# The first MLP's square on ScalarE, and the low parts of the weights' combinations a slot later

## The chip, the core and the metric

The kernel runs on one core of one Trainium2 chip. TensorE (PE in the profile) multiplies, with weight loads shown apart as PEld; VectorE (DVE) and ScalarE (ACT) do the elementwise work; all transfers are issued from the queue of SyncE (SP). The metric is the time of one execution on the device in microseconds (us), lower is better.

## The reference, cut to what matters

```python
batch, n_heads, seq, head_dim, n_pack = 8, 8, 576, 64, 32

p_packed = sm_attn(p, k, v)                    # softmax attention of 32 queries per head
out = sm_attn(q, p_packed, p_packed)           # all 576 positions on the 32 packed ones
x = out.transpose(0, 2, 1, 3).reshape(4608, 512)

h = np.maximum(x @ w_in, 0.0)                  # first MLP, 512 -> 2048 -> 512
x = h * h @ w_out

h = x @ w_in2                                  # second MLP, 512 -> 2048 -> 512
g = h * (1.0 / (1.0 + np.exp(-1.702 * h)))
return g @ w_out2
```

The weights arrive as 64-bit floats (read as int64 pairs of words), everything else as float32.

## The kernel before, in words

**Precision.** Each factor of a large product is kept as a high and a low part: the high part is a copy on ACT into a rounded type, the low part is the source minus the high part on DVE (`split`, lines 76 and 77). `prod` (line 85) then makes three matmuls for one product: high by high, high by low, low by high.

**First stage: attention and first MLP, by slots.** The batch of 8 is cut into halves of 288 positions (`HS`). One slot is one chunk `fc` of 128 of the 2048 hidden features, for one half of one batch: 256 slots in all (`SB`). In slot s the program is written in this order: `gsplit` of slot s+2 (high part on ACT, low part on DVE of the squared relu, tile `gh`), `mm1` of slot s+3 (six matmuls into the PSUM tile `h`, then the relu into `r` on ACT at line 381, then the square into `gf`), `mm2` of slot s (twelve matmuls that add to four accumulators `y`), and then what `plan[s]` holds. Every engine works through its own instructions in this order. `h` has two PSUM buffers, so `mm1` of slot s+5 can't start until all readers of `h` of slot s+3 are done. In slots 0 to 31 (batch 0) and 48 earliest slots in all the square is on ACT (line 384); in the other 208 it is on DVE (line 386), which reads `h` in PSUM a second time: max(h, 0) times r.

After the last chunk of a run (16 slots in most of the stage) the four accumulators are copied to `ysb`: those of even number on ACT (line 416), those of odd number on DVE (line 414). The next run's first `mm2` writes the same four accumulators. Two runs add to an earlier partial sum instead, all on DVE (line 412, `yp`).

**What else the plan holds.** For the next batch, spread over the slots: the packed attention (`s1`, `tr`, `pv`, `t2`), the second softmax for the two halves (`s2a`, `s2b`, `s2c`: transposes on DVE at line 330, maximum at 332, subtraction at 334, the exponential on ACT at 339, then lines 341, 343, 345, 347 and 350 on DVE, and the split of the result at 355 and 357), and four `m_step`, which multiply the packed values into `w_in` (high part on ACT at 366, low part on DVE at 368). So in each batch a half's softmax ends in the slots just before a run does. `interleave` writes out the first part of each planned step and then, in turns, what stands behind each `yield`.

**The second MLP's weights** are prepared in the same slots. Of each pair of 128-row blocks seven combinations of 256 columns are needed. `convert` loads and turns the 64-bit words into floats (lines 118 and 119 on ACT, 123 to 129 on DVE), `unit_sums` makes four sums (line 179), `unit_split` splits each combination into a tile `wc` (high at line 188 on ACT, low at line 190 on DVE) and writes it to DRAM (lines 193 and 195, 112 transfers of 256 KB). `wc` has two buffers. One unit takes eight slots of the list `calm`, which leaves out the slots with s % 16 of 14, 15 and 0, and starts at slot 45; its first slot has no split, the seven others have one each. SP issues these writes in the order of the program, between the loads of k, q, v, weights and raw words.

**Second stage.** The second MLP works on five pairs of column blocks with seven products in place of eight. It reads the weights that the first stage wrote, from slot 248 on; the last combination is made in slot 213.

Of the kernel before, what the change touches and what calls it, by code (L numbers as in the profile page):

```python
# [8 lines left out]
F32 = mybir.dt.float32  # L9
F32R = mybir.dt.float32r  # L10
# [3 lines left out]
AF = mybir.ActivationFunctionType  # L14
ALU = mybir.AluOpType
# [7 lines left out]
P = 128  # L23
HS = S // 2
# [19 lines left out]
def fused_kernel(ctx, tc, qT, kT, vv, pT, w_in, w_out, w_in2, w_out2, out):  # L44
# [7 lines left out]
    nc = tc.nc  # L52
# [26 lines left out]
    def prod(ps, ws, xs, start, stop, more=False):  # L79

        n = 3 * len(ws)
        i = 0
        for (wh, wl), (xh, xl) in zip(ws, xs):
            for w, x in ((wh, xh), (wh, xl), (wl, xh)):
                nc.tensor.matmul(ps, w, x, start=start and i == 0, stop=stop and i == n - 1,  # L85
                                 skip_group_check=more)
                i += 1
# [8 lines left out]
    cv_p = poola("cv", 3)  # L96
# [7 lines left out]
    s2_p = poola("s2", 1)  # L104
# [74 lines left out]
            nc.vector.tensor_tensor(out=t[:, o, :], in0=i0, in1=i1, op=op)  # L179
            yield  # L180

    def unit_split(u, i):

        xa, xb, t = xs[u, 0], xs[u, 1], xs[u, "s"]
        x = {1: xa[:, :256], 2: xb[:, :256], 3: t[:, 3, :], 4: xb[:, 256:], 5: t[:, 0, :], 6: t[:, 1, :], 7: t[:, 2, :]}[i]
        x = x.rearrange("p (c n) -> p c n", c=2)
        o = cv_p.tile([P, 2, 2, P], F32R, tag="o", name=f"wc{u}_{i}", bufs=2)
        nc.scalar.activation(o[:, :, 0, :], x, AF.Copy)
        yield
        nc.vector.tensor_tensor(out=o[:, :, 1, :], in0=x, in1=o[:, :, 0, :].bitcast(F32), op=ALU.subtract)  # L190
        if u < 8:
            q, d = divmod(u, 2)
            nc.sync.dma_start(out=w1_d[:, 2 * q:2 * q + 2, ORDER_A.index(i), d], in_=o.bitcast(F32))
        else:
            nc.sync.dma_start(out=w2_d[:, ORDER_B.index(i), u - 8], in_=o.bitcast(F32))
# [42 lines left out]
    def att_tile(b, alt, name):  # L238

        pool, tag = (mm_p, "mm") if b == 0 and alt else (at_p, "at")  # L240
        return pool.tile([P, 512], F32, tag=tag, name=name)

    def heads(ps, w, x):

        n = None
        for hp in range(4):
            for r in range(2):
                rows = slice(64 * r, 64 * r + 64)
                xx = x(hp)[rows]
                n = xx.shape[-1]  # L250
                nc.tensor.matmul(ps[r][32 * hp:32 * hp + 32, :n], w(hp)[rows], xx, start=True, stop=True)  # L251
# [69 lines left out]
    s2t = {}  # L321
    NB = HS // 32

    def s2a(b, hf):
        ps = [att_tile(b, False, f"s2_{b}_{hf}_{r}") for r in range(2)]
        heads(ps, lambda hp: ppT[b][:, 32 * hp:32 * hp + 32], lambda hp: qt[b, hp][:, hf * HS:(hf + 1) * HS])
        t = s2_p.tile([P, 2 * NB, 32], F32, tag="s2t", name=f"s2t{b}_{hf}", bufs=2)
        st = s2_p.tile([P, 3, 2 * NB, 1], F32, tag="s2st", name=f"s2st{b}_{hf}", bufs=2)
        for r in range(2):
            nc.vector.transpose(out=t[:, r * NB:(r + 1) * NB].rearrange("p n i -> p (n i)"), in_=ps[r][:, :HS])  # L330
            yield
        nc.vector.tensor_reduce(out=st[:, 0], in_=t, axis=AX.X, op=ALU.max)
        yield
        nc.vector.tensor_tensor(out=t, in0=t, in1=st[:, 0].to_broadcast([P, 2 * NB, 32]), op=ALU.subtract)
        s2t[b, hf] = t, st
# [37 lines left out]
    def mm1(b, hf, fc, seg):  # L373
        ps = mm_p.tile([P, 512], F32, tag="mm", name=f"h_{b}_{hf}_{fc}")
        m = M[b, fc // 4]
        c = slice((fc % 4) * P, (fc % 4 + 1) * P)
        a = A[b, hf]
        prod(ps[:, :HS], [(m[:, g, 0, c], m[:, g, 1, c]) for g in range(2)],
             [(a[:, g, 0, :], a[:, g, 1, :]) for g in range(2)], True, True)
        r = g_p.tile([P, HS], F32, tag="r", name=f"r_{b}_{hf}_{fc}")  # L380
        nc.scalar.activation(r, ps[:, :HS], AF.Relu)  # L381
        g = g_p.tile([P, HS], F32, tag="g", name=f"gf_{b}_{hf}_{fc}")
        if b < 1 or b < 2 and fc < 8:
            nc.scalar.activation(g, r, AF.Square)
        else:
            nc.vector.scalar_tensor_tensor(out=g, in0=ps[:, :HS], scalar=0.0, in1=r, op0=ALU.max, op1=ALU.mult)  # L386
        gf[b, hf, fc] = g

    def gsplit(b, hf, fc, seg):
# [221 lines left out]
    def run(item):  # L611
# [6 lines left out]
            (0, 0, 8, 15), (0, 1, 8, 15), (1, 0, 8, 15), (1, 1, 8, 15)]  # L618
    runs += [(b, hf, 0, NFC - 1) for b in range(2, B) for hf in range(2)]
    slots = [(mm1, gsplit, mm2, (b, hf, fc, (f0, f1))) for b, hf, f0, f1 in runs for fc in range(f0, f1 + 1)]  # L620
    SB = len(slots)
    plan = {s: [] for s in range(S0, len(slots))}
    plan_end = {s: 0 for s in plan}

    def at(s, f, *a):
        plan[s].append((f, a))
# [17 lines left out]
    def convert(s):  # L644

        nonlocal nconv
        n = nconv
        nconv += 1
        c, b, a = (cq[i] if 0 <= i < len(cq) else None for i in (n - 2, n - 1, n))
        if c:  # L650
            at(s, lambda: c["use"](c["x"]))
        if a:
            at(s, conv_a, a)
        if b:
            at(s, conv_b, b)
        if 0 <= n - 1 < len(cq):
            plan_end[s] += 1
# [21 lines left out]
    for f, *a in (*loads(0)[:6], (ahead,), loads(0)[6], (ahead,), (load_q, 0, 0, 0), (load_q, 0, 1, 0), (ahead,),  # L679
# [6 lines left out]
        -8: [(tr, 0, 1), (warm, 8), (convert,)],  # L686
        -7: [(convert,), (pv, 0, 0), (pv, 0, 1), (warm, 2), (t2, 0)],
        -6: [(convert,), (s2a, 0, 0)],
        -5: [(s2b, 0, 0), (convert,), (warm, 14)],
        -4: [(convert,), (s2a, 0, 1), (s2c, 0, 0), (warm, 14), (m_step, 0, 0)],  # L690
        -3: [(convert,)],
        -2: [(s2b, 0, 1), (convert,)],
# [7 lines left out]
        6: [(pv, 1, 0), (convert,), (tr, 1, 1)],  # L700
        7: [(convert,), (pv, 1, 1), (t2, 1)],
        8: [(s2a, 1, 0), (convert,)],
        9: [(s2b, 1, 0)],
        10: [(s2c, 1, 0), (convert,)],
# [28 lines left out]
    for b in range(1, B):  # L733
# [20 lines left out]
        for n in range(8):  # L754
            f = n // 2
# [5 lines left out]
    for u in range(2 * KC + 1):  # L761
        s = calm[8 * u:8 * u + 8]
        convert(s[0])
        convert(s[3])
        if u > 0:
            at(s[1], unit_sums, u - 1)
            for j, i in zip(s[1:], (2, 4, 1, 5, 6, 7, 3)):
                at(j, unit_split, u - 1, i)

    at(SB - 2 * NFC, open_b)  # L770

# [23 lines left out]
    for p in range(NP2):  # L795
        t0 = 2 * SL * p
        for c in range(KC):
            u = t0 + 7 * c
# [20 lines left out]
        for c in range(KC):  # L819
            u = t0 + 7 * c  # L820
# [5 lines left out]
        for n in range(14):  # L826
            i, h = ORDER_B[n // 2], n % 2
# [61 lines left out]
```

## Time and profile before

| | |
|---|---|
| Time, median of 3 runs | 1516.89 us (1514.85 to 1519.79) |
| Profiled execution, time | 1515.2 us |
| Profiled execution, span of its instructions | 1513.4 us |
| Granted TensorE clock, mean | 0.982 |
| PE busy | 1454.4 us (96%) |
| DVE busy | 1052.7 us (70%) |
| ACT busy | 760.6 us (50%) |

Busy time is that of instructions on the engine; the idle time of an engine is shown in front of the instruction that ended it, with what released that instruction. A granted clock of 1.00 is 2.4 GHz and 0.50 is 1.2 GHz; a stretch between the two had part of its time at either. Matmuls are pipelined, so their durations overlap.

### The profile page before, as it was taken

The page shows a single profiled execution, that of the slowest core. Times are in us where ns is not written, and L with a number is a line of the kernel's source. Part 1 is how long each engine was busy: PE and PEld are TensorE (multiplying, and loading weights), DVE is VectorE, ACT ScalarE, POOL GpSimd, SP SyncE. Part 2 cuts the span into 40 slices and gives each one's busy share as a digit, 9 for nine tenths or more (in the row PEclk, how much of TensorE's full clock was granted, in tenths as well). Part 3 has the DMA queues.
Part 4 walks back from the last instruction along what each step waited for, and adds up shares of the span by engine and source line. Part 5 has one row for each costly group of instructions (what it writes and reads, how often), then busy time and mean ns, then how long its engine had stood idle before and what let it go on. Part 6 is the DMA issues. An engine that isn't in the chain of part 4 may idle for free.

```text
span 1513.4 us, 25199 instructions
## 1 busy us (share of the span) xinstructions
PE 1454.4 (96%) x9786; PEld 1305.6 (86%) x9786; DVE 1052.7 (70%) x1892; ACT 760.6 (50%) x1552; POOL 0.7 (0%) x6
## 2 busy tenths in 40 slices
PE   7899999899899998999999999999999999999998
PEld 4678988888788888888999888888888889998997
DVE  6898477767768767685446678567757675876675
ACT  4888645445454554554345453454446344534542
POOL 0000000000000000000000000000000000000000
PEclk8899999999999999999999999999999999999999
DMA  8756647466465654643034576667656765675663
GB/s 301 244 175 220 208 165 228 153 221 217 141 214 175 205 185 160 230 136 121 17 143 162 199 259 245 226 211 273 237 207 236 273 223 198 250 267 212 218 243 145
DMA packets 110776, 307.97 MB, mean 203 GB/s; under 512 B 9024, under 2 KB 58176, under 8 KB 96576
## 3 DMA queue, kind: packets, MB, share of 16 engines
q1 hardware_dynamic: 110656, 306.35, 58.4%
q8 instruction: 77, 1.26, 0.3%
q14 instruction: 43, 0.35, 0.1%
HBM read 250.94 MB, written 55.38 MB: 202 GB/s over the span
## 4 chain that ended last, share of the span: by engine, by line
PE 75%; DVE 14%; ACT 4%; DMA 4%; issue 3%; SPq 0%; ACTq 0%; DVEq 0%
PE h L85 32%; PE y L85 20%; PE o L85 19%; DMA w_d<-wc 2%; PE m L251 2%; PE s L251 1%; DVE gh L77 1%; DVE gf L386 1%; DVE yT L480 1%; ACT g L515 1%; DVE y L491 1%; DVE T L510 1%; PE pv L309 1%; DVE M L368 1%; DVE s2t L347 1%
## 5 line engine op out<-in xcount | busy, mean ns | idle before, releaser
L85 PE MATMUL y<-gh,wo 128*128 128x288 f32 x3072 | 462.7, 300 | 17.0 <-DVE ysb L414 11.0
L85 PEld LDWEIGHTS y<-gh,wo 128*128 128x128 f32 x3072 | 433.1, 193 | 21.1 <-DVE ysb L414 12.5
L85 PE MATMUL h<-y,wA 128*128 128x464 f32 (+1 forms) x1680 | 355.6, 371 | 3.0 <-ACT r L553 2.9
L85 PE MATMUL o<-g,wB 128*128 128x464 f32 (+1 forms) x1680 | 354.6, 371 | 0.0
L85 PEld LDWEIGHTS h<-y,wA 128*128 128x128 f32 x1680 | 314.9, 188 | 40.5 <-ACT r L553 4.9
L85 PEld LDWEIGHTS o<-g,wB 128*128 128x128 f32 x1680 | 315.3, 188 | 35.6
L85 PE MATMUL h<-a,M 128*128 128x288 f32 x1536 | 267.0, 310 | 22.5 <-DVE gf L386 14.3
L85 PEld LDWEIGHTS h<-a,M 128*128 128x128 f32 x1536 | 223.4, 195 | 71.7 <-DVE gf L386 25.4
L76 ACT ACTIVATE gh<-gf 128x288 fp32r<-128x288 f32 x256 | 113.0, 442 | 93.8 <-DVE gf L386 93.1
L381 ACT ACTIVATE r<-h 128x288 f32<-128x288 f32 x256 | 103.3, 404 | 89.0 <-PE h L85 88.6
L77 DVE TENSOR_TENSOR gh<-gf,gh 128x288 fp32r<-128x288 f32 x256 | 115.0, 450 | 37.7 <-ACT gh L76 37.6
L561 DVE TENSOR_TENSOR hid<-h,r 128x464 f32<-128x464 f32 (+1 forms) x120 | 76.0, 634 | 77.5 <-PE h L85 66.4
L553 ACT ACTIVATE r<-h 128x464 f32<-128x464 f32 (+1 forms) x120 | 66.5, 554 | 119.3 <-PE h L85 119.3
L386 DVE SCALAR_TENSOR_TENSOR gf<-h,r 128x288 f32<-128x288 f32 x208 | 93.9, 451 | 45.8 <-ACT r L381 45.6
L515 ACT ACTIVATE g<-T 128x928 fp32r<-128x928 f32 (+1 forms) x60 | 58.5, 974 | 126.8 <-DVE T L510 119.7
L571 DVE TENSOR_TENSOR hid<-hid,sg 128x464 f32<-128x464 f32 (+1 forms) x120 | 75.7, 631 | 47.5 <-ACT sg L567 47.5
L491 DVE TENSOR_TENSOR g<-T,g 128x928 fp32r<-128x928 f32 (+1 forms) x60 | 66.7, 1118 | 53.3 <-ACT g L515 52.3
L491 DVE TENSOR_TENSOR g<-hid,g 128x928 fp32r<-128x928 f32 (+1 forms) x80 | 86.0, 1111 | 1.2 <-ACT g L515 1.1
L567 ACT ACTIVATE sg<-hid 128x464 f32<-128x464 f32 (+1 forms) x120 | 70.2, 585 | 30.7 <-DVE hid L561 30.7
L515 ACT ACTIVATE g<-hid 128x928 fp32r<-128x928 f32 (+1 forms) x80 | 74.3, 968 | 20.6 <-PE o L85 20.6
L368 DVE TENSOR_TENSOR M<-m,M 128x512 fp32r<-128x512 f32 x64 | 43.5, 687 | 40.1 <-ACT M L366 39.8
L510 DVE TENSOR_TENSOR T<-hid 128x928 f32<-128x928 f32 (+1 forms) x60 | 66.2, 1111 | 0.0
(97 smaller groups left out, 1022.8 us busy)
## 6 DMA issues: line engine op xcount, KB each, us to landing
wB<-w_d SPq DMA_DIRECT2D x70, 1024.0 KB, 4.7
wA<-w_d SPq DMA_DIRECT2D x40, 1024.0 KB, 4.7
wA<-w_d SPq DMA_DIRECT2D x40, 768.0 KB, 6.4
win<-win_d SPq DMA_DIRECT2D x56, 512.0 KB, 4.8
w_d<-wc SPq DMA_DIRECT2D x112, 256.0 KB, 2.6
k<-in_kT SPq DMA_DIRECT2D x32, 288.0 KB, 4.7
y_d<-ysb SPq DMA_DIRECT2D x16, 576.0 KB, 3.9
v<-in_vv SPq DMA_DIRECT2D x16, 512.0 KB, 5.9
```

What stands on the lines that cost most here:

```text
L76: nc.scalar.activation(hi, src, AF.Copy)
L77: nc.vector.tensor_tensor(out=lo, in0=src, in1=hi.bitcast(F32), op=ALU.subtract)
L85: nc.tensor.matmul(ps, w, x, start=start and i == 0, stop=stop and i == n - 1, skip_group_check=more)
L381: nc.scalar.activation(r, ps[:, :HS], AF.Relu)
L386: nc.vector.scalar_tensor_tensor(out=g, in0=ps[:, :HS], scalar=0.0, in1=r, op0=ALU.max, op1=ALU.mult)
L491: nc.vector.tensor_tensor(out=t[:, :, 1, :n], in0=src, in1=t[:, :, 0, :n].bitcast(F32), op=ALU.subtract)
L510: nc.vector.tensor_tensor(out=t, in0=i0, in1=i1, op=ALU.subtract)
L515: nc.scalar.activation(t[:, :, 0, :PAIRS[p]], gop[p, i, g, "src"], AF.Copy)
L553: nc.scalar.activation(t[:, 0, :n], bank[p, c, "1"][:, :n], AF.Copy)
L561: nc.vector.tensor_tensor(out=hid(p, c, blk), in0=bank[p, c, b][:, :n], in1=part[p, c, r][:, 0, :n], op=ALU.add)
L567: nc.scalar.activation(t, bank[p, c, "1"][:, :n] if blk == 2 else hid(p, c, blk), AF.Sigmoid, scale=GELU)
L571: nc.vector.tensor_tensor(out=hid(p, c, blk), in0=bank[p, c, "1"][:, :n] if blk == 2 else hid(p, c, blk), in1=part.pop((p, c, "sg", blk)), ...
```

## The change

The square of the first MLP is written as a Square activation of `r` on ACT, right behind the relu, in all 256 slots; before, 208 of them had it on DVE, reading `h` and `r`. The tile `wc` gets a third buffer. `unit_split` becomes two steps: `unit_hi` makes the high part in the slot where it was, `unit_lo` makes the low part and issues the write to DRAM in the slot behind it. Two tiles of the second softmax, `s2t` and `s2st`, go from two buffers to one, which makes room for the third `wc`.

```diff
-    def unit_split(u, i):
+    wcs = {}
+
+    def unit_hi(u, i):
 
         xa, xb, t = xs[u, 0], xs[u, 1], xs[u, "s"]
...
-        o = cv_p.tile([P, 2, 2, P], F32R, tag="o", name=f"wc{u}_{i}", bufs=2)
+        o = cv_p.tile([P, 2, 2, P], F32R, tag="o", name=f"wc{u}_{i}", bufs=3)
         nc.scalar.activation(o[:, :, 0, :], x, AF.Copy)
-        yield
+        wcs[u, i] = o, x
+
+    def unit_lo(u, i):
+        o, x = wcs.pop((u, i))
         nc.vector.tensor_tensor(out=o[:, :, 1, :], in0=x, in1=o[:, :, 0, :].bitcast(F32), op=ALU.subtract)
         if u < 8:
             q, d = divmod(u, 2)
...
-        t = s2_p.tile([P, 2 * NB, 32], F32, tag="s2t", name=f"s2t{b}_{hf}", bufs=2)
-        st = s2_p.tile([P, 3, 2 * NB, 1], F32, tag="s2st", name=f"s2st{b}_{hf}", bufs=2)
+        t = s2_p.tile([P, 2 * NB, 32], F32, tag="s2t", name=f"s2t{b}_{hf}", bufs=1)
+        st = s2_p.tile([P, 3, 2 * NB, 1], F32, tag="s2st", name=f"s2st{b}_{hf}", bufs=1)
...
         g = g_p.tile([P, HS], F32, tag="g", name=f"gf_{b}_{hf}_{fc}")
-        if b < 1 or b < 2 and fc < 8:
-            nc.scalar.activation(g, r, AF.Square)
-        else:
-            nc.vector.scalar_tensor_tensor(out=g, in0=ps[:, :HS], scalar=0.0, in1=r, op0=ALU.max, op1=ALU.mult)
+        nc.scalar.activation(g, r, AF.Square)
         gf[b, hf, fc] = g
...
             for j, i in zip(s[1:], (2, 4, 1, 5, 6, 7, 3)):
-                at(j, unit_split, u - 1, i)
+                at(j, unit_hi, u - 1, i)
+                at(j + 1, unit_lo, u - 1, i)
```

## Rows read from the trace of the kernel before

**Rows 1.** Windows: length, busy (and count) by engine, granted clock, DMA share, GB/s.

```profile
36.00:190.00 154.00, 141.73 (x1227) 125.15 (x1227) 118.90 (x251) 116.76 (x273) 0.00 (x0) 0.95 0.65 214
190.00:800.00 610.00, 581.19 (x4937) 532.11 (x4936) 422.49 (x986) 301.71 (x757) 0.00 (x0) 0.97 0.51 169
800.00:1513.40 713.40, 706.11 (x3381) 632.58 (x3379) 489.87 (x610) 327.38 (x493) 0.00 (x0) 1.00 0.62 226
...
120.00:160.00 40.00, 39.42 (x326) 35.79 (x327) 30.64 (x65) 33.01 (x80) 0.00 (x0) 1.00 0.76 246
```

**Rows 2.** Groups, 190 to 800 us: busy, mean ns; idle before, releasers.

```profile
L85 PE MATMUL y<-gh,wo 128*128 128x288 f32 x2504 | 376.7, 300 | 14.3 <-DVE ysb L414 11.0 <-ACT gh L76 3.2
...
L85 PE MATMUL h<-a,M 128*128 128x288 f32 x1242 | 211.5, 306 | 14.5 <-DVE gf L386 14.3
...
L386 DVE SCALAR_TENSOR_TENSOR gf<-h,r 128x288 f32<-128x288 f32 x208 | 93.9, 451 | 45.8 <-ACT r L381 45.6
L76 ACT ACTIVATE gh<-gf 128x288 fp32r<-128x288 f32 x208 | 91.9, 442 | 93.5 <-DVE gf L386 93.1
```

**Rows 3.** Waits, 190 to 800 us: total, times, longest.

```profile
DVE wc L190 <- ACT wc L188: 39.6, 25, 4.2
ACT wc L188 <- DMA w_d<-wc: 37.9, 19, 4.3
```

**Rows 4.** Timeline of DVE: start, duration, instruction, idle before.

```profile
277.52 0.85 DVE L330 STREAM_TRANSPOSE s2t<-s 128x288 f32<-128x288 f32 x2 [1.33 <-PE s L251]
...
292.30 0.76 DVE L341 TENSOR_REDUCE s2st<-s2t 128x18 f32<-128x576 f32 x1
...
295.43 0.45 DVE L386 SCALAR_TENSOR_TENSOR gf<-h,r 128x288 f32<-128x288 f32 x1
295.80 0.81 DVE L414 COPY ysb<-y 128x288 f32<-128x288 f32 x2
```

**Rows 5.** Timeline of PE at five of its waits.

```profile
292.34 1.09 PE L85 MATMUL h<-a,M 128*128 128x288 f32 x6 [1.24 <-DVE gf L386]
...
296.30 1.03 PE L85 MATMUL y<-gh,wo 128*128 128x288 f32 x5 [2.22 <-DVE ysb L414]
...
535.87 1.56 PE L85 MATMUL h<-a,M 128*128 128x288 f32 x5 [2.61 <-DVE gf L386]
...
579.51 1.19 PE L85 MATMUL h<-a,M 128*128 128x288 f32 x6 [1.98 <-DVE gf L386]
...
590.03 2.15 PE L85 MATMUL y<-gh,wo 128*128 128x288 f32 x9 [2.10 <-DVE ysb L414]
```

**Rows 6.** Windows around two falls of the clock, which is third from the end.

```profile
294.00:300.00 6.00, 3.78 (x18) 3.71 (x18) 3.76 (x9) 1.36 (x4) 0.00 (x0) 0.75 0.29 101
...
392.00:400.00 8.00, 5.78 (x27) 5.75 (x27) 4.84 (x11) 2.81 (x7) 0.00 (x0) 0.57 0.21 74
```

**Rows 7.** Timeline of ACT in a slot that has the square there.

```profile
132.65 0.39 ACT L381 ACTIVATE r<-h 128x288 f32<-128x288 f32 x1
133.07 0.45 ACT L384 ACTIVATE gf<-r 128x288 f32<-128x288 f32 x1
133.42 0.61 ACT L149 ACTIVATE wo<-x_wo 128x512 fp32r<-128x512 f32 x1
```

**Rows 8.** Timelines of ACT and DVE around two waits for wc.

```profile
532.12 0.42 ACT L188 ACTIVATE wc<-x_p 128x256 fp32r<-128x256 f32 x1 [2.02 <-DMA w_d<-wc]
...
533.25 0.40 ACT L381 ACTIVATE r<-h 128x288 f32<-128x288 f32 x1
...
535.36 0.45 DVE L386 SCALAR_TENSOR_TENSOR gf<-h,r 128x288 f32<-128x288 f32 x1
...
576.33 0.43 DVE L190 TENSOR_TENSOR wc<-sum,wc 128x256 fp32r<-128x256 f32 x1 [2.55 <-ACT wc L188]
```

**Rows 9.** Groups, 36 to 190 us, where the square is on ACT.

```profile
L85 PE MATMUL y<-gh,wo 128*128 128x288 f32 x551 | 83.9, 303 | 2.7 <-ACT ysb L416 2.7
...
L85 PE MATMUL h<-a,M 128*128 128x288 f32 x286 | 52.8, 319 | 6.5 <-ACT a L355 3.1 <-ACT M L366 1.2 <-DVE M L368 1.1
```

## The prediction

> **What bounds the kernel now.** I read the windows first, by stage [rows 1]. From 800 us on PE is busy for 706.11 of 713.40 us at a clock of 1.00, and the change touches nothing there: that part keeps its time. Up to 190 us the square is on ACT already. So the change acts from 190 to 800 us. There PE is busy for 581.19 of 610 us, which leaves 28.8 us of waits, and its clock averages 0.97. DVE has 422.49 us of work (69%), ACT 301.71 (49%). No engine but PE is full, so only a wait that reaches PE is worth anything, and the clock that falls behind such waits.
>
> The groups of that stage say what the waits are [rows 2]: 14.3 us of `h` waiting for the square on DVE (line 386 is the last reader of the PSUM buffer), and 14.3 us of `y` at the starts of runs, 11.0 put down to DVE's copies of the accumulators (line 414) and 3.2 to ACT. ACT itself waits 93.1 us for DVE's square before the high part of `gh`: it costs nothing directly, but it shows which engine is late. A second source stands in the waits [rows 3]: ACT waits 37.9 us in 19 places for a write of `wc` to land, and DVE then waits 39.6 us for ACT's high part.
>
> Where DVE is late can be seen in its timeline before the end of a run [rows 4]. From 277.52, where PE's scores release it, to the copy of `ysb` at 295.80 it works without a break: two softmax chains, conversions, low parts, squares. PE meanwhile waits 1.24 us for `h` and 2.22 us for `y` [rows 5]. The same picture stands before the end of four runs (near 296, 394, 490 and 684 us); the fifth, at 590, has another beginning (below). The windows then show the clock [rows 6]: 0.75 in 294 to 300 us, 0.57 in 392 to 400. Lost clock is (1 - 0.75) x 6 = 1.5 us and (1 - 0.57) x 8 = 3.4 us. There are seven falls in the stage: five of the short kind (near 200, 297, 536, 580 and 590 us, 1.5 to 1.7 us each) and two of the long (near 392 and 682), some 15.2 us together; the stage's mean of 0.97 says 18 to its last digit. So waits and clock in the stage hold 28.8 + 15.2 = 44.0 us: no gain can be larger.
>
> **The squares.** DVE loses 208 of 451 ns [rows 2]; in its chains the next instruction starts 0.37 us behind a square (295.43 to 295.80 [rows 4]), so 77 us in all, and its share falls to (422.5 - 77) / 610 = 57%. ACT gains 208 squares. A square there takes 0.45 us, starts 0.42 us after its relu, and the next starts 0.35 us later [rows 7]: between 73 and 94 us, since it can't overlap the relu it reads; I take 94, and ACT comes to 65%. What hides it: ACT's 93.1 us of waits for DVE's square go, for its own square is ready in its own order. Behind the square on ACT stand the rest of the slot's ACT work and the next high part; where ACT then waits for DVE's line 334 or for PE's `m`, it waited before too, so there the square fills a wait. A new coupling: the square writes one of three `gf` buffers, whose last reader is DVE's low part of three slots earlier; DVE must be some two slots late before that holds ACT, which no row shows.
>
> The Trainium skill (ScalarE: Activation LUTs, What ACT_TABLE_LOAD costs) says that back-to-back activations overlap by about 93 ns; by that the squares would cost ACT 208 x 0.35 = 73 us, the lower end above. The trace shows such an overlap behind the square and nearly none between relu and square.
>
> **What the squares give.** (a) `h` is now free when ACT's relu ends. The program has the low part of `gh` one instruction ahead of the old square on DVE, and PE needs it 0.8 us later (six matmuls), so DVE may be about 1.2 us later than before until PE stops. Single waits of `h` outside the places below come to about 3.2 of the 14.3 us; I count 2.5 as gained (0 to 3.2). (b) Before the end of a run DVE's own chain still decides. Of the squares between 277.52 and 295.80 four count, for line 341 at 292.30 waits for ACT's exponential and the square in between is free; 4 x 0.37 = 1.48 us. One low part of `wc` more falls into the chain, since each moves a slot on: 0.33 (its row has 0.43 long [rows 8]). That is 1.15 for each of four runs, 4.6 in all. The other 2.5 us or so of each stay, as one wait of `y` for `ysb`. The bounds are 0 and 14 (all of it). (c) Two runs start by adding to `yp` on DVE: one square each and a little, 0.7.
>
> **The combinations.** Before, the high part in slot j needs the buffer of slot j-2, whose write is issued in slot j-2. Now it needs that of slot j-3, whose low part and write come in slot j-2. In slots the distance is the same: the third buffer only makes up for the later low part. It is the order that changes: the low part doesn't wait for a high part of its own slot. Rows 8 show both kinds. At 532.12 ACT waits 2.02 us for a write that stands on SP behind the next batch's four loads of k; those loads are still ahead of one slot's write in each batch, so this wait mostly stays. PE's 2.61 us at 535.87 [rows 5] shrinks anyway, because the relu at 533.25 frees `h` 2.1 us earlier than the square at 535.36; then the low part just ahead of that square stops `y`. I count 1.6 (0.5 to 2.6). At 576.33 DVE stands 2.55 us behind a high part that waits for its buffer, with a softmax chain queued behind; that goes, for the low part then is one whose high part is a slot old. PE's 1.98 at 579.51 goes, and of its 2.10 at 590.03 I count 1.7. Together 5.3 us (bounds 0.5 and 6.7). The moved writes pass no transfer that anyone reads in the first stage, and the last is written some 34 slots before it is read. The single buffers of `s2t` and `s2st` cost nothing: writer and last reader are both on DVE, one slot or more apart.
>
> **The clock.** The falls near 536, 580 and 590 lie behind waits that go or halve: 5.1 us. Of the other four, 10.1 us, their waits shrink by a third; I take half, 5 (0 to 10).
>
> **Sum.** 2.5 + 4.6 + 0.7 + 5.3 + 10.1 = 23.2 us; new waits behind a busier ACT, which no row shows, 2 (0 to 8): 21 us. Profiled time 1515.2 us (span 1513.4 and 1.8 around it), so 1494 us. The median of the runs shown, 1516.89, lies 0.1% above the profiled one; I leave that out. The forecast's own range is 1483 to 1504.
>
> **Rivals.** *The waits only move* (chance 0.20). DVE's softmax chain, the low parts and the copies still run one behind another; `h` stops waiting and `y` waits instead, the writes of `wc` land in the same slots, and the clock falls as before. Then (b) and (c) alone are left, 5 us: 1510. For it: the 2.22 us waits are on DVE's copies, not its squares, and the distance of the writes in slots doesn't change. Against: 579.51, where DVE's wait for ACT's high part is plainly the cause.
>
> *All of it goes* (0.13): DVE at 57% catches up everywhere and the clock stays up. 44 less the 6 or so that the four runs keep: 38 us, 1477.
>
> *ACT becomes the one that is late* (0.12, the slower side). In its one queue the relu that frees `h`, the square, the high part and the copies of `ysb` stand behind waits for DVE's softmax, for `m`, and for writes of `wc`. From 36 to 190 us, with squares on ACT, PE's waits name ACT: 3.1 + 1.2 + 2.7 = 7.0 us in 154 [rows 9]. Over 610 us that is 28 us, in place of `h`'s 14.3: 1515.2 + 13 = 1528. It decides from where ACT, after such a wait, still has more than two slots' work before it; against it, ACT was at 76% there and comes to 65% here, and in 120 to 160 us PE is busy for 39.42 of 40 with ACT at 33.01 [rows 1]. The Trainium skill (ScalarE: Activation LUTs, Rules for kernel authors) gives relu, max and multiply to VectorE rather than ScalarE, which speaks for this rival; by the rows a square takes the two engines the same time, 451 ns [rows 2] and 0.45 us [rows 7], so the rule's reason isn't seen here.
>
> **From chances to numbers.** Forecast 0.55, the others as given. About 0.3% (4.5 us) is what a measurement of this kernel can tell from no change. The forecast, the large gain and a third of "only move" are faster: 0.55 + 0.13 + 0.07 = 0.75; the rest of "only move" and a little of the ACT rival same, 0.14; slower 0.11. The range for 8 in 10 runs from the large gain to "only move": 1476 to 1511.
>
> **What would show it.** In the profile after: no wait of `h` for DVE; line 386 gone and 256 squares on ACT; DVE near 345 us and ACT near 395 us in the stage; the waits of `y` for `ysb` still there, 1.5 to 2.7 us at four run ends; ACT's waits for writes of `wc` under 37.9 us but not gone, DVE's for ACT's high part (39.6) gone; two to four falls of the clock in place of seven. The prediction is wrong if `h` waits for ACT's relu by more than a few us, if the run-end waits keep their full length, or if the clock falls as often as before.

## The result, and the profile after

The changed kernel takes 1501.43 us (median of 4 runs, 1500.98 to 1502.14) against 1516.98 us for the kernel before (median of 4); the ratio is 0.9897, 95% interval 0.988 to 0.9914. It is 15.6 us faster, where 21 us were forecast; 1501.43 lies in the range of 1476 to 1511 and inside the forecast's own one of 1483 to 1504. The profiled execution took 1500.98 us, with a span of 1498.8 us.

The windows of the changed stage, which now ends some 15 us earlier, and those behind five run ends (columns as in rows 1):

```profile
190.00:790.00 600.00, 579.03 (x4976) 533.77 (x4975) 348.72 (x783) 389.75 (x970) 0.00 (x0) 0.98 0.53 172
...
384.00:394.00 10.00, 6.41 (x35) 5.95 (x34) 6.95 (x15) 4.05 (x11) 0.00 (x0) 0.83 0.41 142
476.00:486.00 10.00, 7.65 (x45) 7.19 (x44) 7.12 (x15) 4.15 (x11) 0.00 (x0) 0.84 0.31 113
572.00:582.00 10.00, 6.17 (x27) 5.94 (x28) 5.74 (x14) 5.34 (x14) 0.00 (x0) 0.66 0.31 111
668.00:676.00 8.00, 6.12 (x33) 5.90 (x34) 3.69 (x9) 3.74 (x10) 0.00 (x0) 0.79 0.27 96
...
290.00:300.00 10.00, 7.61 (x37) 7.38 (x38) 5.71 (x14) 5.49 (x15) 0.00 (x0) 0.66 0.25 87
```

PE's waits in the stage are 600 - 579.0 = 21.0 us, where they were 28.8 [rows 1]. DVE fell to 348.7 us (58%) and ACT rose to 389.8 (65%), as worked out. The clock still falls, now five times and always at a run's end: 3.4 (290 to 300), 1.7, 1.6, 3.4 and 1.7 us are lost, 11.8 in all, where it was 15.2. Waits and clock together went from 44.0 to 32.8 us, 11.2 of the stage's some 15; the rest does not stand in these rows.

The groups of the stage say which waits are left:

```profile
L85 PE MATMUL y<-gh,wo 128*128 128x288 f32 x2531 | 377.9, 298 | 19.7 <-ACT ysb L418 9.7 <-DVE ysb L416 7.9 <-DVE yp L414 2.1
...
L85 PE MATMUL h<-a,M 128*128 128x288 f32 x1242 | 208.3, 304 | 1.3 <-ACT r L386 1.3
...
L76 ACT ACTIVATE gh<-gf 128x288 fp32r<-128x288 f32 x208 | 90.6, 436 | 1.5
```

`h` waits 1.3 us, where it waited 14.3 [rows 2], and ACT is idle 1.5 us in front of the high part, where it was 93.5. But `y` waits 19.7 us where it waited 14.3: 9.7 for ACT's copies of the accumulators and 7.9 for DVE's. From the waits of the same stage, DVE's longest and ACT's for the transfers of `wc`:

```profile
DVE gh L77 <- ACT gh L76: 104.4, 82, 5.3
...
ACT wc L190 <- DMA w_d<-wc: 27.3, 15, 4.3
```

ACT still waits 27.3 us for the writes (37.9 in rows 3); DVE's 39.6 us for ACT's high part of `wc` are gone, and DVE now waits 104.4 us for the high part of `gh` instead.

The run end near 290 us in the timelines, ACT first, then DVE, then PE (start, duration, instruction, idle before):

```profile
288.70 0.69 ACT L344 ACTIVATE s2t<-s2t 128x576 f32<-128x576 f32 x1 [3.42 <-DVE s2t L339]
289.29 0.42 ACT L76 ACTIVATE gh<-gf 128x288 fp32r<-128x288 f32 x1
289.62 0.39 ACT L386 ACTIVATE r<-h 128x288 f32<-128x288 f32 x1
290.05 0.44 ACT L388 ACTIVATE gf<-r 128x288 f32<-128x288 f32 x1
290.39 0.69 ACT L418 ACTIVATE ysb<-y 128x288 f32<-128x288 f32 x2
```

```profile
292.55 0.81 DVE L416 COPY ysb<-y 128x288 f32<-128x288 f32 x2
```

```profile
290.84 0.66 PE L85 MATMUL y<-gh,wo 128*128 128x288 f32 x3 [1.82 <-ACT ysb L418]
293.05 1.33 PE L85 MATMUL y<-gh,wo 128*128 128x288 f32 x4 [1.55 <-DVE ysb L416]
```

ACT is idle for 3.42 us, because the exponential stands in its queue and waits for DVE's softmax chain. Behind it come high part, relu, square, and only then the copies for which PE has waited 1.82 us. Then the softmax runs on through DVE until its own copies at 292.55, and PE waits another 1.55 us. That is 3.37 us, where it was 1.24 + 2.22 at this place [rows 5] and a first small one of 0.50.

One pair of waits has another source, near 340 us:

```profile
337.24 0.42 ACT L190 ACTIVATE wc<-sum 128x256 fp32r<-128x256 f32 x1 [3.06 <-DMA w_d<-wc]
```

```profile
338.82 1.05 PE L85 MATMUL h<-a,M 128*128 128x288 f32 x6 [1.31 <-ACT r L386]
340.85 1.86 PE L85 MATMUL y<-gh,wo 128*128 128x288 f32 x12 [0.97 <-ACT ysb L418]
```

Here ACT is late because it waited for a write of `wc`, not for the softmax. Before, PE waited 1.35 us at this place (342.08 us). The clock does not fall behind the pair.

### The profile page after: what moved, and what is told of

The parts are those of the page before. It is cut to its first block, busy times and chain, and to the rows that moved or that the text cites. A ratio compares the mean times of both kernels' runs of the same rounds, so it can differ in the third digit from the quotient of the medians.

```text
span 1498.8 us, 25122 instructions
## 1 busy us (share of the span) xinstructions
PE 1447.4 (97%) x9786; PEld 1301.4 (87%) x9786; DVE 974.5 (65%) x1684; ACT 846.3 (56%) x1760; POOL 0.7 (0%) x6
## 4 chain that ended last, share of the span: by engine, by line
PE 78%; DVE 12%; ACT 6%; issue 2%; DMA 2%; SPq 0%; ACTq 0%; DVEq 0%
PE h L85 34%; PE y L85 23%; PE o L85 16%; PE m L256 2%; ACT g L517 2%; DVE T L512 2%; DVE g L493 1%; PE s L256 1%; DVE yT L482 1%; DVE y L493 1%; PE pv L314 1%; DMA k<-in_kT 1%; DVE s2st L337 1%; DVE gh L77 1%; DVE s2t L335 1%
## 5 line engine op out<-in xcount | busy, mean ns | idle before, releaser
L85 PEld LDWEIGHTS y<-gh,wo 128*128 128x128 f32 x3072 | 430.9, 192 | 27.5 <-ACT ysb L418 15.8
L85 PE MATMUL h<-a,M 128*128 128x288 f32 x1536 | 263.7, 307 | 9.8 <-ACT a L360 3.9
L388 ACT ACTIVATE gf<-r 128x288 f32<-128x288 f32 x256 | 113.9, 445 | 8.1
```

## The experiments

Each was timed beside the kernel before, in three sets: e1 to e4 (before: 1517.43 us), e5, e6, e7 and e9 (1518.86), e11 and e12 (1516.94). All times are medians. The kernel before differs by up to 1.9 us between the sets, so a difference between kernels of two sets is uncertain by at least that much.

| kernel | squares | `wc` buffers | low part | softmax, second half | us | ratio to before (95%) |
|---|---|---|---|---|---|---|
| changed kernel | ACT | 3 | slot later | before run end | 1501.43 | 0.9897 (0.988 to 0.9914) |
| e1_square | ACT | 2 | own slot | before | 1503.21 | 0.9901 (0.988 to 0.9922) |
| e2_split | DVE | 3 | slot later | before | 1517.07 | 1.0002 (0.9987 to 1.0017) |
| e3_lo_back | ACT | 3 | own slot | before | 1493.73 | 0.9844 (0.982 to 0.9868) |
| e4_two | ACT | 2 | slot later | before | 1530.73 | 1.0088 (1.006 to 1.0116) |
| e9_buffer | DVE | 3 | own slot | before | 1507.93 | 0.9921 (0.9905 to 0.9936) |
| e6_copies_act | ACT | 3 | own slot | before, copies on ACT | 1477.89 | 0.973 (0.9714 to 0.9746) |
| e7_square_next | ACT, slot later | 3 | own slot | before | 1493.32 | 0.9831 (0.9814 to 0.9847) |
| e5_softmax_late | ACT | 3 | own slot | behind | 1467.16 | 0.966 (0.9644 to 0.9677) |
| e11_dve_late | DVE | 3 | own slot | behind | 1481.37 | 0.9768 (0.9744 to 0.9792) |
| e12_after_late | ACT | 3 | slot later | behind | 1470.68 | 0.9706 (0.968 to 0.9732) |

**e1_square: the square alone.**

```diff
 (of the kernel before)
-        if b < 1 or b < 2 and fc < 8:
-            nc.scalar.activation(g, r, AF.Square)
-        else:
-            nc.vector.scalar_tensor_tensor(out=g, in0=ps[:, :HS], scalar=0.0, in1=r, op0=ALU.max, op1=ALU.mult)
+        nc.scalar.activation(g, r, AF.Square)
```

> Only the square moves to ACT; combinations, their two buffers and the softmax tiles are as before. Theory (the square is what kept h waiting, the combinations are a source of their own): h waits for DVE go from 14.3 us to under 2, DVE's wait for ACT's high part of wc stays near 40 us and ACT's for the writes near 38 us; 8 to 11 us of the 15.6 us, so 1506 to 1509 us. Rival (the two parts only work together, since a late high part holds DVE's whole queue): 1512 us or more, with y waiting where h did.

1503.21 us, 14.2 us faster than before: the square alone brings nearly all of the change's gain, and more than the theory's 8 to 11. From its waits in 190 to 785 us:

```profile
DVE wc L190 <- ACT wc L188: 54.7, 43, 4.7
...
ACT wc L188 <- DMA w_d<-wc: 34.0, 19, 3.7
...
PE h L85 <- ACT r L381: 2.1, 2, 1.3
```

DVE waits longer for ACT's high part than before (54.7 us, 39.6 before) and the kernel is faster all the same: the length of that wait alone does not say what it costs. `y` now waits 10.1 us for ACT's copies, and some waits of `h` have only turned into these. Near 525 us, which was 536 before, `h` waits 0.77 us for the relu (2.61 for the square before), and `y` 0.97 us behind it. At the run end near 575 us `y` waits 1.90 and 1.68 us, where `h` waited 1.98 near 580 and `y` 2.10 near 590 before.

**e2_split: the combinations alone.** The changed kernel with the four lines of the old square put back.

> Only the combinations change (third buffer, low part a slot later, single softmax tiles); 208 squares stay on DVE. Theory (the low part's wait for a high part of its own slot is a source of its own): DVE's wait for the high part goes from 39.6 us to about 0, the 1.98 and 2.10 us waits near 580 and 590 us go, the h waits of about 1.2 us at the run ends stay; 4 to 7 us faster than before, 1510 to 1513 us. Rival (write and reuse are as many slots apart as before, so nothing changes): 1515 to 1519 us.

1517.07 us, no change in time: the rival holds. Its waits in 190 to 785 us show where the removed wait went:

```profile
DVE gh L77 <- ACT gh L76: 53.2, 94, 4.2
...
DVE M L373 <- ACT M L371: 41.6, 30, 4.5
...
ACT wc L190 <- DMA w_d<-wc: 32.1, 16, 4.3
...
PE h L85 <- DVE gf L391: 14.3, 17, 2.5
...
PE y L85 <- DVE ysb L419: 11.5, 5, 2.5
```

The line of `gh` in the kernel before, in the same window:

```profile
DVE gh L77 <- ACT gh L76: 30.0, 72, 0.8
```

DVE's wait for the high part of `wc`, 39.6 us, is gone from the list, but `h` waits the same 14.3 us in total. DVE no longer stands in front of the low part of `wc`; it stands in front of the low parts of `gh` (23.2 us more) and of `M` (41.6 us, 30.2 before), whose high parts are in ACT's queue behind the same write. So 34.6 of the 39.6 us came back.

PE's timeline, place by place, shows that the same total is a gain and a loss:

```profile
344.76 1.35 PE L85 MATMUL h<-a,M 128*128 128x288 f32 x6 [2.45 <-DVE gf L391]
...
539.59 1.05 PE L85 MATMUL h<-a,M 128*128 128x288 f32 x6 [0.49 <-DVE gf L391]
...
587.23 1.44 PE L85 MATMUL h<-a,M 128*128 128x288 f32 x6 [1.98 <-DVE gf L391]
```

The wait near 536 us went from 2.61 to 0.49, and no fall of the clock is left there. The 1.98 us near 580 is gone too: DVE runs its softmax chain from 576.12 us while ACT waits for the write until 578.55. But 1.98 us of `h` stand at the run end behind it (587.23), the 1.35 us at 342 became 2.45 with a new fall of the clock, and `y` waits 2.45 us at four run ends where it waited 2.22.

**e3_lo_back: the low part back in its slot, three buffers.**

```diff
 (of the changed kernel)
-        wcs[u, i] = o, x
-
-    def unit_lo(u, i):
-        o, x = wcs.pop((u, i))
+        yield
...
-                at(j + 1, unit_lo, u - 1, i)
```

> As the changed kernel, but the low part and the write stand again in the slot of their high part; three buffers stay. Theory (the low part's place is what helps, not the buffer): DVE waits for the high part again, 30 us or more, ACT's wait for the writes falls from 27.3 us to under 15 because the distance is three slots; 2 to 5 us slower than the changed kernel, 1503 to 1506 us. Rival (the buffer is what helps): 1498 to 1501 us.

1493.73 us, 7.7 us faster than the changed kernel: the theory falls, the rival holds. From its waits in 190 to 785 us:

```profile
DVE wc L192 <- ACT wc L190: 22.1, 35, 2.3
...
PE y L85 <- DVE ysb L413: 7.9, 5, 1.7
PE y L85 <- ACT ysb L415: 6.7, 5, 2.2
...
ACT wc L190 <- DMA w_d<-wc: 2.4, 2, 1.5
```

With the write three slots ahead of the reuse, ACT's waits for it fall from 27.3 to 2.4 us. DVE waits for ACT's high part again, 22.1 us (the theory had 30 or more), and the kernel is faster all the same.

**e4_two: two buffers, low part a slot later.** The changed kernel with `bufs=2` for `wc`.

> As the changed kernel, but wc has two buffers, with the low part still a slot later. Theory (the third buffer only makes up for the later low part): a high part then needs a write that was issued one slot before; a write takes 3.6 us to land and a slot about 2.9, so ACT waits 1 to 3 us for most of 112 high parts, 100 us or more in total, and PE stops behind it: 1515 us or more. Rival (PE has two slots of slack and ACT's waits stay hidden): within 3 us of the changed kernel, 1499 to 1505 us.

1530.73 us, 29.3 us slower than the changed kernel and slower than before, as the theory said, though ACT's waits are fewer and longer than the theory's (39 places, up to 7.4 us). Its waits in 190 to 785 us:

```profile
ACT wc L190 <- DMA w_d<-wc: 98.5, 39, 7.4
PE h L85 <- ACT r L386: 13.9, 8, 2.5
```

**e9_buffer: the third buffer alone.** The kernel before with the third buffer and the single softmax tiles (e3_lo_back with the old square).

> The kernel before with the third buffer of wc (and the single softmax tiles) and nothing else; squares on DVE, the low part in its own slot. Theory (while h waits for DVE's squares, ACT's waits for the writes are not what ends last): ACT's wait for the writes falls from 37.9 us to under 10, the time to 1512 to 1517 us. Rival (the buffer has a gain of its own, as with the squares on ACT, where it is 9.5 us): 1506 to 1510 us.

1507.93 us, 10.9 us faster than before: the rival holds, the buffer has a gain of its own. Its waits in 190 to 785 us:

```profile
PE y L85 <- DVE ysb L416: 11.0, 5, 2.2
PE h L85 <- DVE gf L388: 9.7, 15, 1.3
...
ACT wc L190 <- DMA w_d<-wc: 5.0, 3, 2.8
```

So with three buffers the later low part costs 1517.07 - 1507.93 = 9.1 us with the squares on DVE, and 7.7 us with them on ACT; by the ratios of the table, each against the kernel before of its own set, it is about 12 and 8.

**e6_copies_act, on top of e3_lo_back: all copies at a run's end on ACT.**

```diff
-                elif d % 2 and b > 1:
+                elif False:
```

> On top of e3_lo_back, all four copies of the accumulators at a run's end are on ACT; the softmax stays where it was. Theory (DVE's copies stand behind its chain, ACT's behind the exponential alone, which ends some 1.5 us earlier): y's waits for DVE go from 7.9 us to 0, those for ACT from 6.7 to 8 to 10 us; 4 to 8 us faster than e3_lo_back: 1486 to 1490 us. Rival (ACT is as late as DVE, four copies in a row take as long): 1492 to 1496 us.

1477.89 us, 15.8 us faster than e3_lo_back, more than the theory's 4 to 8. The waits of `y` in 190 to 785 us are these two, and the window of the stage has a clock of 1.00 where e3_lo_back has 0.98:

```profile
PE y L85 <- ACT ysb L415: 6.7, 5, 2.2
...
PE y L85 <- DVE yp L411: 2.1, 1, 2.1
```

```profile
190.00:785.00 595.00, 586.17 (x5054) 540.63 (x5054) 346.06 (x772) 405.64 (x1008) 0.00 (x0) 1.00 0.54 179
```

DVE's 7.9 us are gone, ACT's 6.7 did not grow, and about as much again came back with the clock: one fall in place of five in this stage, 1.7 us lost in place of 11.9 (added up in windows of 2 us).

**e7_square_next, on top of e3_lo_back: the square in front of the next high part.**

```diff
         nc.scalar.activation(r, ps[:, :HS], AF.Relu)
-        g = g_p.tile([P, HS], F32, tag="g", name=f"gf_{b}_{hf}_{fc}")
-        nc.scalar.activation(g, r, AF.Square)
-        gf[b, hf, fc] = g
+        gf[b, hf, fc] = r
...
-        split(t[:, 0, :], t[:, 1, :], gf.pop((b, hf, fc)))
+        g = g_p.tile([P, HS], F32, tag="g", name=f"gf_{b}_{hf}_{fc}")
+        nc.scalar.activation(g, gf.pop((b, hf, fc)), AF.Square)
+        split(t[:, 0, :], t[:, 1, :], g)
```

> On top of e3_lo_back, the square stands in front of the next high part instead of right behind its relu, so that a run's end has ACT's copies ahead of the square. Theory (the square itself holds those copies for 0.45 us at each of five run ends): y's waits for ACT go from 6.7 us to about 4.5, those for DVE stay; 1 to 3 us faster: 1491 to 1493 us. Rival (the copies wait for the exponential, and the square was free): 1493 to 1496 us, as the high part and DVE's low part come 0.45 us later in every slot.

1493.32 us, the same as e3_lo_back within what two sets can tell; `y` waits 6.7 us for ACT and 7.9 for DVE as there, so the theory's 4.5 us did not come. It tells less than it was meant to, as ACT's timeline at a run's end shows: another square, that of the slot before, now stands between the exponential and the copies.

```profile
289.21 0.68 ACT L341 ACTIVATE s2t<-s2t 128x576 f32<-128x576 f32 x1 [3.60 <-DVE s2t L336]
289.80 0.43 ACT L389 ACTIVATE gf<-r 128x288 f32<-128x288 f32 x1
...
290.90 0.70 ACT L415 ACTIVATE ysb<-y 128x288 f32<-128x288 f32 x2
```

What the square itself costs in front of the copies stays open.

**e5_softmax_late, on top of e3_lo_back: the second half's softmax behind the run's end.**

```diff
-                     (10, s2a, 0), (11, s2b, 0), (13, s2c, 0), (13, s2a, 1), (14, s2b, 1), (17, s2c, 1)]
+                     (10, s2a, 0), (11, s2b, 0), (13, s2c, 0), (17, s2a, 1), (18, s2b, 1), (20, s2c, 1)]
```

> On top of e3_lo_back, the second softmax of a batch's second half is planned behind the end of the run (its three steps in slots 17, 18 and 20 in place of 13, 14 and 17). Theory (what is left of y's waits at the run ends, 6.7 us for ACT's copies and 7.9 us for DVE's, comes from the softmax chain that stands ahead of the copies on both engines): both together under 4 us, at most two falls of the clock in the stage, 12 to 22 us faster than e3_lo_back: 1472 to 1482 us. Rival (relu, square and four copies between two runs are enough to stop PE): the waits stay, 1491 to 1496 us.

1467.16 us, 26.6 us faster than e3_lo_back and 51.7 faster than before. The window, and all of PE's waits that the profile lists in 190 to 785 us:

```profile
190.00:750.00 560.00, 559.34 (x4919) 516.03 (x4918) 339.00 (x774) 387.23 (x962) 0.00 (x0) 1.00 0.55 183
```

```profile
PE y L85 <- DVE gh L77: 0.4, 1, 0.4
PE m L253 <- DMA win<-win_d: 0.2, 1, 0.2
```

No wait at a run's end is left, and no fall of the clock. This is the fastest of the versions.

**e11_dve_late: e5_softmax_late with the old square.**

> As e5_softmax_late, with the 208 squares back on DVE. Theory (two sources: the softmax chain keeps y's copies late, the squares on DVE keep h late also away from the run ends): no waits of y at the run ends, h still waits for the square for 4 us or more and the clock falls once or more; 5 to 14 us slower than e5_softmax_late: 1472 to 1481 us. Rival (h waited for the square only because the softmax chain had made DVE late): 1466 to 1470 us, and the square's move is worth nothing once the chain is moved.

1481.37 us, 14.2 us slower than e5_softmax_late by the medians and about 16 by the ratios: the rival falls, and the two sources hold, at or above the upper end of the theory's 5 to 14. The theory's fall of the clock did not come: `y` no longer waits, `h` does, and the window keeps a clock of 1.00.

```profile
PE h L85 <- DVE gf L388: 10.6, 12, 1.6
```

```profile
190.00:785.00 595.00, 584.24 (x5029) 535.72 (x5028) 431.51 (x999) 311.15 (x770) 0.00 (x0) 1.00 0.54 176
```

**e12_after_late: the changed kernel with the softmax behind the run's end.**

> The changed kernel (low part and write a slot later, three buffers, squares on ACT) with the softmax of the second half behind the run's end as in e5_softmax_late. Theory (the later low part costs through ACT's waits of some 27 us for the writes, which reach PE only where ACT is late already): 2 to 6 us slower than e5_softmax_late, 1469 to 1473 us, with waits of h for ACT's relu at one or two places. Rival (its price is fixed, as between e3_lo_back and the changed kernel, 7.7 us): 1474 to 1477 us.

1470.68 us, 3.5 us slower than e5_softmax_late by the medians, as the theory said, but about 7 by the ratios to the kernel before of each set, so the time does not rule out the rival's 7.7. In 190 to 785 us:

```profile
ACT wc L190 <- DMA w_d<-wc: 27.4, 17, 4.4
...
PE h L85 <- ACT r L386: 1.8, 2, 1.3
...
PE y L85 <- ACT ysb L418: 1.4, 2, 1.0
```

ACT waits as long for the writes as in the changed kernel, but less of it reaches PE: the later low part adds 3.2 us of waits for ACT here (1.8 + 1.4), and added 4.3 to e3_lo_back (`y` 9.7 for 6.7, and 1.3 of `h`).

## Why the prediction was right, and where its sum was off

**What bounds the kernel** was read rightly: no engine but PE is full, PE's waits in 190 to 800 us and the clock behind them are nearly all that can be won, and e5_softmax_late, which has next to none of either, is 51.7 us faster than before by the medians. The 44.0 us that I called the most to be had were worked out from one profiled execution; from that to the profiled one of e5_softmax_late it is 1515.2 - 1467.16 = 48.0 us, 4 more. e11_dve_late shows such a rest without any fall of the clock: its profiled execution is 15.9 us longer than that of e5_softmax_late (1483.06 and 1467.16), and PE's waits in it are 10.6 us. So more is lost with the waits than the rows give as idle time; in what, stays open.

**The squares' cost** came out as worked out. Over the whole execution DVE has 974.5 us where it had 1052.7, 78 less (77 forecast), and ACT 846.3 where it had 760.6, 86 more (73 to 94). In the run end above the square starts 0.43 us after its relu and the next instruction 0.34 us after the square. The Trainium skill (ScalarE: Activation LUTs, Rules for kernel authors) gives relu and multiply to VectorE; here the square is worth 14.2 us on ScalarE with the run ends late (e1_square against before) and 14 to 16 without (e11_dve_late against e5_softmax_late). The square takes about as long on either engine; what counts is which engine `h` has to wait for.

**(a) `h` waits for no square on DVE.** Right: 14.3 us of these waits went to 1.3, now for ACT's relu. But `y` waits 19.7 us where it waited 14.3, so all waits fell by 28.8 - 21.0 = 7.8 us, where the sum had 2.5 + 4.6 + 0.7 + 5.3 - 2 = 11.1. e1_square shows that the square alone brings 14.2 us of time, against 7.8 that the sum gave (a), (b) and (c), or some 13 with the 5 us of clock at the run ends. The part of it that the square does at the places counted under the combinations is small: near 536 us 2.61 us of waits became 1.74, and 4.08 near 580 and 590 became 3.58.

**(b) The run ends.** The mechanism was right: the waits that are left at the run ends are those behind the softmax chain, and moving the chain removes them (e5_softmax_late). The size was too good. Counting all waits of `h` and `y` of 0.3 us or more from the softmax chain on, the five run ends had 3.96, 4.34, 2.88, 4.08 and 4.00 us before, and have 3.37, 3.59, 2.35, 3.93 and 3.36 now: 2.7 us less of 19.3, where 4.6 were expected at four of them and 3.7 at the one of 580 and 590. That is close to one of the prediction's own signs of being wrong, that the run-end waits keep their full length. Near 490 the picture was also not the same as at the other three: the waits of `h` there were 0.30 and 0.36 us, not some 1.24, and the clock did not fall. What the step missed is that ACT's copies are held by the same chain, through the exponential in ACT's queue (3.42 us idle). Before, `h` stopped PE first and so hid it: PE's first matmuls on `y` start at 293.41, behind `h`, when ACT's copies were under way.

```profile
292.96 0.70 ACT L416 ACTIVATE ysb<-y 128x288 f32<-128x288 f32 x2
```

Once `h` no longer waits, `y` waits for ACT (9.7 us, of which 0.97 near 340) and then for DVE (7.9). This is a part of the rival in which the waits only move, though the squares' gain outweighed it.

**The combinations.** This step failed: 5.3 us and the clock behind them were expected from "the low part doesn't wait for a high part of its own slot", and e2_split, which has this part alone, is no faster. At the places that the step named, 536 and 580 us, the waits did go, or nearly, in e2_split; ACT's wait at 532, which was to stay mostly, went with them. What the step left out is what comes elsewhere: 1.10 us and a fall of the clock near 344, and 1.98 us of `h` at 587; the 0.23 us more at each of four run ends stood under (b), as 0.33. The clock's falls cost 17.1 us in e2_split where they cost 15.3 before (added up in windows of 2 us). The working had said itself that in slots the distance from write to reuse is the same, so that the third buffer only makes up for the later low part; e4_two shows what the later low part costs without the buffer. The gain that it then gave to the order is not there in the total: 34.6 of DVE's 39.6 us come back at the next instructions that need the same ACT queue. Alone, the third buffer is worth 10.9 us with squares on DVE and 9.5 with them on ACT (e9_buffer; e1_square to e3_lo_back), and the later low part takes about 9 and 8 of it back. So the change held a gain and its loss, and the term should have been near 0 for the two together.

**The clock.** 10.1 us were expected back, 3.4 came (15.2 to 11.8), with five falls where two to four were named. The falls that are left follow the run-end waits, which stayed.

**New waits behind ACT**, 2 us in the sum, were the copies' 9.7 us, mostly in place of waits of `h` and of `y` for DVE.

**The slower rival** (ACT late by 13 us) did not come true, though in its form it did: `y` waits for ACT at run ends. ACT was late there because it waited for DVE (near 340 us for a write), not because it was full.

**The sum.** That 21 us came near the 15.6 measured is in part luck. The combinations and the clock behind them were 10.4 us of the sum, and e2_split shows nothing of them in the total; the waits and the clock that did go make 11.2 us. Of the 14.2 us between the two profiled executions (1515.2 and 1500.98) the other 3 stand in no term of the sum.

## What to carry to other kernels

A wait that is removed from one reader of a queue can come back at the next instruction that needs the same queue (34.6 of 39.6 us here); ask what the event is that is late, not who stands first behind it. A step moved a slot later and a buffer more cancel out when the buffer's reuse is counted in slots from the transfer: count the distance from the issue of the transfer to the reuse before and after. And where an engine's short copies free what the bottleneck needs next, plan long chains of dependent work behind them: moving the second half's softmax past the run's end was worth 26.6 us here, more than the change.

## What the runs showed of the hardware

The clock was worth at least as much as the waits in front of it. From e3_lo_back to e6_copies_act PE lost 7.9 us of waits and the kernel 15.8 us: the stage's granted clock went from 0.98 to 1.00, and what its falls cost from 11.9 to 1.7 us. The waits for ACT's copies are the same in both at all five run ends (0.52 to 2.25 us). Without DVE's 1.55 us behind them the clock fell at one of the five (0.79 from 378 to 386 us, behind the 2.25), with it at each. The length of one wait does not decide it alone: the kernel before waits 2.22 us at 490 and keeps a clock of 1.00 from 484 to 496 us, and e11_dve_late has twelve waits of up to 1.64 us in the stage and no fall.
